# Reordering the first batch of a fused attention and feed-forward kernel: tan row by transposes, other dummy matmuls, no gates ahead of weight loads

**Chip, cores, metric.** The kernel runs on one core of a Trainium2 chip. The metric is the device time of one execution in microseconds (us), smaller is better; medians of several runs are quoted. Nearly all runs are of state "fast"; the slow ones (more than 1.5% above the fastest run of their kernel) are 7 of 19 of b_tiny, 2 of 22 of b_nogates, and one each of b_dum and b_best_slots. The ratios leave them out.

## The reference

Eight batches of eight heads, 576 positions, 64 features per head. A linear attention with cosine weights, then a feed-forward layer with 512 inputs and 2048 hidden units:

```python
theta = pi / 2 * pos / S;  c, s = cos(theta), sin(theta)
q_p = concat(relu(q) * c, relu(q) * s);  k_p = concat(relu(k) * c, relu(k) * s)
kv  = einsum('bhsf,bhsd->bhfd', k_p, v);  z = sum(k_p, axis=2)
x   = einsum('bhsf,bhfd->bhsd', q_p, kv) / (einsum('bhsf,bhf->bhs', q_p, z) + 1e-6)
h   = x @ w_in                            # (4608, 512) @ (512, 2048)
out = (h / (1 + exp(-beta * h))) @ w_out
```

## The kernel before

The matmuls of the feed-forward layer fill TensorE (PE) for most of the time: 250.8 of the span's 299.4 us by the page, and PE is busy for 96% of it in all. The attention of batch b+1 is worked in between the matmuls of a chunk of 512 tokens. Only the first batch has nothing to hide behind: loads, casts, transposes, kv products, numerators and division come one after another before the first hidden matmul can start. I call this stretch the ramp. Its order, with cuts:

```python
warm_pe(78, 40)                       # 78 dummy matmuls on zeros, 40 columns
q_relu(0, 0, "act")                   # query cast (relu, fp32 -> bf16), heads 0,1 of each half
# tan row: ones (64x128) times diag(tan), two fp32 matmuls, ACT copies to tanr
...
q_relu(0, 1, "dve")
warm_pe(5, 128)
q_turn_pe(0, 0, 4)                    # 9 transposes on PE, then ACT copies and DVE tan products
warm_pe(4, 128)
take = q_turn_pe(0, 1, 2, hold=True)
warm_pe(9)                            # 9 dummies of 512 columns
...
v_scale(0, 1, 0, eng="pool")          # v * sin on GpSimd
v_scale(0, 0, 0)                      # v * cos on DVE
k_relu(0, 0, 2, "act")                # key cast
...
kv_mm(0, 0, 6)                        # 36 matmuls: first kv product
...
nc.sync.dma_start(out=gate, in_=rk[0:1, 0, 0, 0:2])   # gate: SP waits until this key is cast
load_w("in", 1)
nc.sync.dma_start(out=gate, in_=rk[0:1, 0, 3, 0:2])   # second gate
load_w("in", 2)
load_w("in", 3)
...                                   # numerators (72 matmuls), second kv product (36),
...                                   # numerators (72), division, 8 transposes
h_mm(0, 0, (0, 1))                    # first hidden matmuls
x_turn_pe(0, 0, 4, 4, ("dve",), (1,)) # transposes of the second head pair
h_mm(0, 1, (0, 1))
x_turn_pe(0, 4, 8, 5, ("act",), (1,))
...
for i in range(1, 4):                 # DVE casts w_in blocks 1 to 3, behind the xt copies
    ... cast_win(i, gj, "dve", ...)
```

A matmul is two PE instructions, a weight load and the matmul itself (the page counts 3042 matmuls and 3068 weight loads); this will matter.

## Time and profile before

| | before |
|---|---|
| median of the three runs given | 299.19 us (298.54 to 300.53) |
| the run that was profiled | 301.22 us, span of its trace 299.4 us |
| DVE starts the w_in casts | 20.70 us |
| first w_out matmul (end of the ramp and of the first hidden tiles) | 37.81 us |

The last two rows are read from the timelines of DVE and PE. After the first w_out matmul, PE is busy nearly without a break (254.5 of the 261.2 us from 37.81 to 299.0), so what the ramp gains or loses is carried to the end. The second row deserves a look that I did not give it: the profiled run is 2 us slower than the median.

### The profile page before, as it was taken

What the parts mean: (1) busy time and instruction counts of PE and PEld (TensorE: products, weight loads), DVE (VectorE), ACT (ScalarE), POOL (GpSimd) and SP (SyncE); (2) the same over time, 40 slices, a digit from 0 to 9 for tenths busy, and PEclk for the clock granted to TensorE, in tenths of its full rate; (3) what the DMA queues carried; (4) which work ended last, traced back from release to release, by engine and by line L of the source; (5) the groups of instructions that cost most, each with busy time, mean ns of one, the idle gap of its engine ahead of it and who ended that gap; (6) DMA issues with size and microseconds to landing.
All of it is one profiled execution on the core that took longest, in us unless ns stands there. A gap on an engine that the chain in (4) does not pass through costs nothing.

```text
span 299.4 us, 7162 instructions
## 1 busy us (share of the span) xinstructions
PE 286.8 (96%) x3042; PEld 143.7 (48%) x3068; DVE 113.8 (38%) x282; ACT 141.4 (47%) x224; POOL 74.0 (25%) x88
## 2 busy tenths in 40 slices
PE   7959999999999999999999999999999999999994
PEld 6633455445544554455445544554455444444443
DVE  3869856591860077006800680059004000000000
ACT  6645765475128512860276117611761178128511
POOL 1550000516156014701270147014701210000000
PEclk9987999999999999999999999999999999999999
DMA  7999999769699349943995299419301920131032
GB/s 244 384 341 340 390 388 391 217 138 396 123 187 376 126 63 189 345 182 66 192 315 207 48 196 342 189 39 177 86 2 20 158 48 0 37 70 35 0 72 70
DMA packets 50264, 53.82 MB, mean 180 GB/s; under 512 B 30888, under 2 KB 31160, under 8 KB 50232
## 3 DMA queue, kind: packets, MB, share of 16 engines
q1 hardware_dynamic: 47512, 46.01, 51.7%
q0 software_dynamic: 2688, 7.34, 10.5%
q8 instruction: 24, 0.39, 0.6%
q14 instruction: 8, 0.07, 0.1%
q10 hardware_dynamic: 32, 0.01, 0.0%
HBM read 36.71 MB, written 9.44 MB: 154 GB/s over the span
## 4 chain that ended last, share of the span: by engine, by line
PE 92%; DVE 3%; ACT 2%; issue 1%; DVEq 0%; ACTq 0%
PE ps L374 42%; PE ps L399 40%; PE ps L289 3%; PE ps L268 3%; PE ps L415 1%; DVE qs L226 1%; PE ps L348 1%; DVE vb L213 1%; ACT g_t L381 1%; PE ps L432 1%; PE ps L238 1%; ACT xt L353 1%; ACT L151 0%; DVE xs L311 0%; PE ps L424 0%
## 5 line engine op out<-in xcount | busy, mean ns | idle before, releaser
L374 PE MATMUL ps<-xt,win 128*128 128x512 bf16 x576 | 130.4, 384 | 2.5 <-ACT xt L353 1.1
L399 PE MATMUL ps<-wout,g_t 128*128 128x512 bf16 x536 | 120.4, 379 | 2.3 <-issue 1.5
L381 ACT ACTIVATE g_t<-ps,beta 128x512 bf16<-128x512 f32 x144 | 98.7, 688 | 37.7 <-PE ps L374 37.7
L374 PEld LDWEIGHTS <-win 128*128 128x128 bf16 x576 | 56.2, 99 | 70.4 <-issue 4.3
L399 PEld LDWEIGHTS <-g_t 128*128 128x128 bf16 x560 | 53.9, 98 | 64.3 <-issue 0.5
L394 POOL DMA_DIRECT2D out_dram<-o_sb x56 | 35.3, 634 | 148.7 <-ACT o_sb L405 148.7
L405 ACT COPY o_sb<-ps 128x512 f32<-128x512 f32 x35 | 20.5, 586 | 99.6 <-PE ps L399 99.6
L226 POOL TENSOR_TENSOR qs<-qt,tanr 128x1152 bf16<-128x1152 bf16 x12 | 29.2, 2452 | 9.1 <-DVE vb L223 8.4
L280 DVE CAST kv<-ps 128x520 bf16<-128x520 f32 x7 | 4.9, 698 | 68.1 <-PE ps L268 68.1
L418 DVE COPY o_sb<-ps 128x256 f32<-128x256 f32 x1 | 0.4, 425 | 63.2 <-PE ps L415 63.2
L311 DVE TENSOR_TENSOR xs<-ps,rden 128x768 bf16<-128x768 f32 (+3 forms) x24 | 22.3, 935 | 1.0 <-DVE rden L304 0.2
L223 DVE TENSOR_SCALAR vb<-raw_v,cos 128x256 bf16<-128x256 f32 x63 | 17.1, 346 | 0.9 <-DMA raw_v<-in_v_dram 0.9
L300 DVE TENSOR_TENSOR den<-ps,eps 128x12 f32<-128x12 f32 (+3 forms) x25 | 4.1, 162 | 33.5 <-PE ps L289 33.4
L223 DVE TENSOR_SCALAR vb<-raw_v,sin 128x256 bf16<-128x256 f32 x54 | 14.7, 346 | 0.0
L289 PEld LDWEIGHTS <-qt 64*64 64x64 bf16 x576 | 10.5, 105 | 4.2 <-issue 4.2
L289 PE MATMUL ps<-kv,qt 64*64 64x65 bf16 x576 | 11.6, 195 | 0.2 <-ACT kv L278 0.2
L289 PE MATMUL ps<-kv,qs 64*64 64x65 bf16 x576 | 11.5, 193 | 0.0
L198 DVE TENSOR_SCALAR qb<-raw_q 128x1152 bf16<-128x1152 f32 x15 | 10.6, 747 | 1.3 <-DMA raw_q<-in_q_dram 1.3
L289 PEld LDWEIGHTS <-qs 64*64 64x64 bf16 x576 | 10.5, 105 | 0.0
L268 PEld LDWEIGHTS <-rk 64*64 64x64 bf16 x576 | 8.6, 106 | 3.9 <-issue 3.3
L268 PE MATMUL ps<-vb,rk 64*64 64x130 bf16 x576 | 10.2, 218 | 0.3 <-DVE vb L213 0.2
L108 DVE CAST win<-w_stage 64x512 bf16<-64x512 f32 (+2 forms) x20 | 10.0, 502 | 0.4
(58 smaller groups left out, 101.9 us busy)
## 6 DMA issues: line engine op xcount, KB each, us to landing
raw_v<-in_v_dram SPq DMA_DIRECT2D x7, 1152.0 KB, 11.4
raw_k<-in_k_dram SPq DMA_DIRECT2D x7, 1152.0 KB, 14.3
raw_q<-in_q_dram SPq DMA_DIRECT2D x7, 1152.0 KB, 7.3
out_dram<-o_sb POOLq DMA_DIRECT2D x56, 128.0 KB, 3.6
w_stage<-in_moe_w_out_dram SPq DMA_DIRECT2D x4, 1024.0 KB, 9.8
w_stage<-in_moe_w_in_dram SPq DMA_DIRECT2D x3, 1024.0 KB, 6.6
out_dram<-o_sb SPq DMA_DIRECT2D x14, 128.0 KB, 2.4
raw_q<-in_q_dram SPq DMA_DIRECT2D x2, 576.0 KB, 3.9
```

The source lines that it names most:

```text
L108: nc.vector.tensor_copy(o, a)
L198: nc.vector.tensor_scalar(dst, src, scalar1=0.0, scalar2=None, op0=ALU.max)
L223: nc.vector.tensor_scalar(o, a, scalar1=t[:, n : n + 1], scalar2=None, op0=ALU.mult)
L226: eng.tensor_tensor(dst.rearrange("q n (g p) -> q n g p", g=2), src.rearrange("q n (g p) -> q n g p", g=2), tanr[:, n0:n1].unsqueeze(2).to ...
L268: nc.tensor.matmul(t[jj * HP : (jj + 1) * HP, g], lhsT=rk[hs, n, 2 * jp + jj, :], rhs=vb[hs, n, 2 * jp + jj].rearrange("q s e -> q (s e)") ...
L289: nc.tensor.matmul(ps[cols, bank + jj, slot * E : (slot + 1) * E], lhsT=(qt, qs)[cs][rows, jp, n, cols], rhs=kv[rows, g, jp, cs, :], start ...
L311: nc.vector.tensor_tensor(o.rearrange("q j n s d -> q j (n s) d"), nv[:, :, a:z, :, 0:D].rearrange("q j n s d -> q j (n s) d"), rden[:, :, ...
L374: nc.tensor.matmul(ps[:, h_bank(c, jt)], lhsT=win[jt // 4][:, mi, (jt % 4) * P : (jt % 4 + 1) * P], rhs=xt[:, :, jp, g * HP : (g + 1) * HP ...
L381: nc.scalar.activation(g_t, ps[:, h_bank(c, jt)], AF.Silu, scale=beta[:, jt : jt + 1])
L394: eng.dma_start(out=out_v[bb, n][:, m0:m1], in_=o_sb[hf * HP : (hf + 1) * HP, m0:m1])
L399: nc.tensor.matmul(o_ps, lhsT=gs[c, jt][:, tt * P : (tt + 1) * P], rhs=wout[jt // 4][:, jt % 4, :], start=(jt == 0), stop=(jt == JT - 1))
L405: nc.scalar.copy(o_sb, o_ps)
```

## The change

The intent is to keep PE busy through the ramp, where the trace of before has the clock at 0.50 from 19.89 to 26.72 us, and to shorten the query path: the tan row comes from nine small transposes, queries are cast on VectorE, dummies fill every gap, and the weight loads are issued without waiting. The diff, cut to its core:

```diff
-    warm_pe(78, 40)
-    q_relu(0, 0, "act")
+    warm_pe(74, 32)
...
-        nc.tensor.matmul(ps[:, bank, 0 : (n1 - n0) * HP], lhsT=ones,
-                         rhs=tdiag[:, n0:n1, :], start=True, stop=True)
+        for n in range(n0, n1):
+            nc.tensor.matmul(ps[:, bank, (n - n0) * HP : (n - n0 + 1) * HP],
+                             lhsT=tan9[0:HP, n : n + 1].to_broadcast([HP, P]), rhs=identf,
+                             is_transpose=True, start=(n == n0), stop=(n == n1 - 1))
...
+    q_relu(0, 0)
...
+    warm_pe(36, 32)
+    take0 = q_turn_pe(0, 0, 4, hold=True)
+    take0("act", 0)
+    take0("act", 1)
+    take0("dve", 1)
+    q_relu(0, 1)
+    take0("dve", 0)
...
-    warm_pe(5, 128)
-    q_turn_pe(0, 0, 4)
-    warm_pe(4, 128)
+    warm_pe(24, 32)
     take = q_turn_pe(0, 1, 2, hold=True)
-    warm_pe(9)
+    warm_pe(64, 32)
+    warm_pe(5)
...
-    k_relu(0, 0, 2, "act")
+    k_relu(0, 0, 2, "act", 0, 5)
+    k_relu(0, 0, 2, "dve", 5, NQ)
...
-    nc.sync.dma_start(out=gate, in_=rk[0:1, 0, 0, 0:2])
-    load_w("in", 1)
-    nc.sync.dma_start(out=gate, in_=rk[0:1, 0, 3, 0:2])
-    load_w("in", 2)
-    load_w("in", 3)
-    warm_pe(1, bank=1)
+    for i in range(1, 4):
+        load_w("in", i)
+    warm_pe(2)
...
     x_mul(got, 0, 4)
+    x_mul(got3, 7, NQ)
     x_mul(got, 4, 7)
-    x_mul_act(got2, 7)
+    warm_pe(4, bank=3)
     h_mm(0, 0, (0, 1))
-    x_turn_pe(0, 0, 4, 4, ("dve",), (1,))
+    warm_pe(1, bank=2)
     h_mm(0, 1, (0, 1))
-    x_turn_pe(0, 4, 8, 5, ("act",), (1,))
-    x_mul_act(got2, 8)
+    x_turn_pe(0, 0, 4, 4, ("act",), (1,))
     h_mm(0, 2, (0, 1))
+    x_turn_pe(0, 4, 8, 5, ("dve",), (1,))
```

Batch 1's transposes and numerators also move one slot later in the first chunk. Also left out of the cut: two ninths of the first product of v with sin go from GpSimd to ScalarE (ACT), and the cast of the last w_out block moves two slots. I call everything above the gates the first half of the change, the rest the second half.

More of the change, by code (lines that the diff above doesn't have):

```diff
@@ L140 @@
                        allow_small_or_imprecise_dtypes=True)
+    zeros = const.tile([P, 512], BF16, name="zeros")
+    nc.vector.memset(zeros[:, 0:P], 0.0)
     halfpi = const.tile([P, 1], FP32, name="halfpi")
@@ L153 @@
     nc.scalar.activation(warm, zero_b, AF.Silu, scale=1.0)
-    zeros = const.tile([P, 512], BF16, name="zeros")
-    nc.vector.memset(zeros, 0.0)
-    ones = const.tile([HP, P], FP32, name="ones")
-    nc.vector.memset(ones, 1.0)
+    nc.vector.memset(zeros[:, P:512], 0.0)
     identf = const.tile([HP, HP], FP32, name="identf")
@@ L162 @@
     make_identity(nc, ident)
-    gate = const.tile([1, 2], BF16, name="gate")
     vb = one.tile([P, NQ, 4, 2, E], BF16, name="vb")
@@ L176 @@
     nc.vector.tensor_tensor(tan9, eps9, sin9, op=ALU.mult)
-    tdiag = const.tile([HP, NQ, HP], FP32, name="tdiag")
-    nc.vector.tensor_tensor(
-        tdiag, identf.unsqueeze(1).to_broadcast([HP, NQ, HP]),
-        tan9[0:HP].unsqueeze(2).to_broadcast([HP, NQ, HP]), op=ALU.mult)
     nc.vector.tensor_scalar(eps9, eps9, scalar1=EPS, scalar2=None, op0=ALU.mult)
@@ L427 @@
     rbeta = const.tile([P, JT], FP32, name="rbeta")
-    warm_pe(78, 40)
-    q_relu(0, 0, "act")
+    warm_pe(74, 32)
     for bank, n0, n1 in ((6, 0, 5), (7, 5, NQ)):
-        nc.tensor.matmul(ps[:, bank, 0 : (n1 - n0) * HP], lhsT=ones,
-                         rhs=tdiag[:, n0:n1, :], start=True, stop=True)
+        for n in range(n0, n1):
+            nc.tensor.matmul(ps[:, bank, (n - n0) * HP : (n - n0 + 1) * HP],
+                             lhsT=tan9[0:HP, n : n + 1].to_broadcast([HP, P]), rhs=identf,
+                             is_transpose=True, start=(n == n0), stop=(n == n1 - 1))
+    nc.tensor.transpose(ps[:, 1, 0:JT], beta16, identf[0:JT, 0:JT])
     for bank, n0, n1 in ((6, 0, 5), (7, 5, NQ)):
-        nc.scalar.copy(tanr[:, n0:n1, :].rearrange("q n p -> q (n p)"), ps[:, bank, 0 : (n1 - n0) * HP])
-    nc.tensor.transpose(ps[:, 1, 0:JT], beta16, identf[0:JT, 0:JT])
+        nc.vector.tensor_copy(tanr[:, n0:n1, :].rearrange("q n p -> q (n p)"), ps[:, bank, 0 : (n1 - n0) * HP])
+    nc.vector.tensor_copy(beta, ps[:, 1, 0:JT])
+    q_relu(0, 0)
     nc.vector.tensor_copy(ps[:, 0, 0:NQ], cos9)
     nc.vector.tensor_copy(ps[:, 0, 16 : 16 + NQ], sin9)
-    nc.vector.tensor_copy(beta, ps[:, 1, 0:JT])
+    warm_pe(36, 32)
[5 more added lines that the diff above has]
+    take0("dve", 0)
     nc.vector.reciprocal(rbeta, beta)
-    q_relu(0, 1, "dve")
-    warm_pe(5, 128)
-    q_turn_pe(0, 0, 4)
-    warm_pe(4, 128)
+    warm_pe(24, 32)
     take = q_turn_pe(0, 1, 2, hold=True)
-    warm_pe(9)
+    warm_pe(64, 32)
+    warm_pe(5)
     take("act", 0)
-    v_scale(0, 1, 0, eng="pool")
+    take("dve", 1)
+    v_scale(0, 1, 0, 0, 7, eng="pool")
+    v_scale(0, 1, 0, 7, NQ, eng="act")
     v_scale(0, 0, 0)
-    k_relu(0, 0, 2, "act")
-    take("dve", 1)
+    k_relu(0, 0, 2, "act", 0, 5)
+    k_relu(0, 0, 2, "dve", 5, NQ)
     take("dve", 0)
@@ L471 @@
         num_mm(n, 0, 2, n)
+    warm_pe(2, bank=1)
     kv_mm(0, 1, 6)
-    warm_pe(2, bank=1)
     got2 = x_rden(4, 0, 7, NQ, (0,))
@@ L479 @@
     x_mul_act(got2, 8)
+    warm_pe(2, bank=1)
     for n in range(7, NQ):
@@ L488 @@
     x_turn_pe(0, 0, 8, 2, jps=(0,))
-    got2 = x_rden(6, 0, 7, NQ, (1,))
+    got3 = x_rden(6, 0, 7, NQ, (1,))
     got = x_rden(0, 0, 0, 7, (1,))
     x_mul(got, 0, 4)
+    x_mul(got3, 7, NQ)
     x_mul(got, 4, 7)
-    x_mul_act(got2, 7)
+    warm_pe(4, bank=3)
     h_mm(0, 0, (0, 1))
-    x_turn_pe(0, 0, 4, 4, ("dve",), (1,))
+    warm_pe(1, bank=2)
     h_mm(0, 1, (0, 1))
-    x_turn_pe(0, 4, 8, 5, ("act",), (1,))
-    x_mul_act(got2, 8)
+    x_turn_pe(0, 0, 4, 4, ("act",), (1,))
     h_mm(0, 2, (0, 1))
+    x_turn_pe(0, 4, 8, 5, ("dve",), (1,))
     h_mm(0, 3, (0, 1))
@@ L530 @@
         22: lambda: (kv_mm(1, 0, 6), kv_mm(1, 1, 6), q_relu(1, 1), kv_take((0, 1), 6)),
-        24: lambda: (cast_wout(3, "aadd"), takes.append(q_turn_pe(1, 0, 4, hold=True))),
-        25: lambda: (takes.append(q_turn_pe(1, 1, 6, hold=True)),
+        25: lambda: (takes.append(q_turn_pe(1, 0, 4, hold=True))),
+        26: lambda: (takes.append(q_turn_pe(1, 1, 6, hold=True)), cast_wout(3, "aadd"),
                      [takes[jp](e, i) for jp in range(2)
                       for e, i in (("act", 0), ("dve", 1), ("act", 1), ("dve", 0))]),
-        28: lambda: (num_seven(0, 4), num_seven(1, 6), x_mul(x_rden(4, 0, 0, 7, (0,)), 0, 7)),
-        29: lambda: (x_turn_pe(1, 0, 7, 4, ("act",), (0,)), x_mul(x_rden(6, 0, 0, 7, (1,)), 0, 7)),
+        29: lambda: (num_seven(0, 4), num_seven(1, 6), x_mul(x_rden(4, 0, 0, 7, (0,)), 0, 7)),
+        30: lambda: (x_turn_pe(1, 0, 7, 4, ("act",), (0,)), x_mul(x_rden(6, 0, 0, 7, (1,)), 0, 7)),
         31: lambda: ([h_mm(1, jt, (0, 1)) for jt in range(2)], x_turn_pe(1, 0, 7, 5, ("dve",), (1,)),
```

## The prediction

> **What bounds the kernel now.** I began with the page's slices: from slice 8 on (after some 52 us) PE is at 9 in all but the last, at full clock, and no part of the change that costs much time lies there. So the case is the ramp. Next I cut the ramp into windows at the points where PE's state changes (columns: stretch, its length, busy us and instructions of PE, weight loads, DVE, ACT, POOL, granted clock, DMA share, GB/s).
>
> ```profile
> 17.07:19.80 2.73, 0.70 (x4) 0.29 (x3) 1.14 (x2) 1.43 (x3) 2.41 (x6) 1.00 0.83 249
> 19.80:22.43 2.63, 1.68 (x9) 0.97 (x9) 1.97 (x7) 0.86 (x3) 0.00 (x0) 0.52 1.05 406
> 22.43:26.72 4.29, 4.29 (x11) 1.50 (x11) 4.11 (x9) 1.52 (x3) 0.00 (x0) 0.50 1.02 359
> 26.72:37.81 11.09, 11.03 (x53) 4.94 (x52) 10.01 (x24) 9.06 (x15) 0.00 (x0) 1.00 0.99 368
> ```
>
> The reader is to see a nearly idle PE (0.70 us of 2.73), then half clock for 6.9 us. PE worked 1.68 + 4.29 = 5.97 us at half clock, so the throttle itself cost at most 5.97 / 2 = 3.0 us. Third, PE's timeline over that stretch (start, length, instruction, idle time before it and what ended it):
>
> ```profile
> 18.17 0.59 PE L374 MATMUL ps<-xt,win 128*128 128x512 bf16 x2 [1.10 <-ACT xt L353]
> 18.60 0.27 PE L348 MATMUL ps<-ident,xs 128*128 128x128 bf16 x2
> 19.86 0.40 PE L348 MATMUL ps<-ident,xs 128*128 128x128 bf16 x2 [0.99 <-issue]
> 20.05 1.06 PE L374 MATMUL ps<-xt,win 128*128 128x512 bf16 x2
> 20.90 0.63 PE L348 MATMUL ps<-ident,xs 128*128 128x128 bf16 x4
> 22.43 5.72 PE L374 MATMUL ps<-xt,win 128*128 128x512 bf16 x16 [0.89 <-ACT xs L321]
> ```
>
> Three gaps: 1.10 us for an xt copy, 0.99 us for "issue" in the middle of four transposes, and 0.89 us for the ACT piece of the last division. Fourth, DVE over the same stretch: it waits for those transposes, copies xt, and then casts weights without a break.
>
> ```profile
> 20.36 0.42 DVE L355 COPY xt<-ps 128x512 bf16<-128x512 bf16 x1 [2.15 <-PE ps L348]
> 20.70 10.45 DVE L108 CAST win<-w_stage 64x256 bf16<-64x256 f32 x20
> ```
>
> The casts end at 31.15, while the last four hidden tiles start at about 37.81 - 4 x 0.864 = 34.4 us (0.864: four matmuls at 0.216 apart; w_out matmuls start at 37.81). So DVE has 3.2 us of slack, and that is all that a faster PE can take before it waits for casts.
>
> The 0.99 us on issue needs an owner. Both transposes after it carry no wait. The page's DMA table has a queue of instructions; the same view in windows of 0.3 us finds its first fetches at 11.4, 17.4, 23.8 and 47.6 us (the first two shown).
>
> ```profile
> q8 instruction: 24, 0.39, 0.6%
> ...
> q8 instruction: 1, 0.02, 20.4%
> ...
> q8 instruction: 1, 0.02, 23.0%
> ```
>
> 24 fetches of 16 KB against 3042 + 3068 PE instructions: 6110 / 24 = 255 each. Counting PE's records, the stall falls after the 703rd. Going back 256 gives number 447, where the first numerator matmuls stop from 13.61 to 13.74, and 191, passed at 8.3. The fetch after each comes late: 8.3 to 11.4, 13.7 to 17.4, 19.9 to 23.8, so 3.1 to 3.9 us[...], lasts 1.0 to 1.1, and PE goes on 1.3 us after its end (12.4 to 13.74, 18.5 to 19.86). A block of 256 PE instructions thus cannot be had in the ramp in less than 5.5 to 6.1 us. I hold this for the owner of that gap; it is a reading of three coincidences, not proved.
>
> [...]
>
> **The change, part by part.**
> 1. Tan row. Out go tdiag (0.75 us on DVE) and a ones matmul, four passes from 4.29 to 6.58. In come nine fp32 transposes. From the one weight load of that kind, 0.18 to 0.33 us, I estimate 0.21 x 9 = 1.9 us, from 3.45 (tan ready 3.38) to about 5.5. Copies go from ACT to DVE (2 x 0.4). Gain in the row: about 1 us, but only 0.4 us at the first query transpose (7.54 to about 7.1), as DVE now has the copies, the beta copy and the query cast (0.69, ACT took 1.16) in line.
> 2. The rest of the head before 14 us gains nothing at the end: the last key piece lands at 13.93 us (ACT waits 0.38 for it) and kv of the second head pair cannot be done before about 15.1; it is done at 15.24 now. 0.1 us at most.
> 3. Dummies. Before: 99 in the whole ramp. After: 74 + 36 + 24 + 64 tiny and 16 long, 214 in all. Tiny ones are cheap in time (0.036 us each at 40 columns) but each is two instructions.
> 4. The last division moves from ACT to DVE: removes the 0.89 us gap, adds some 0.3 us on DVE.
> 5. Without gates the DMA dip at 17.0 to 18.5 (149 GB/s against 385: 0.9 us of transfer) goes. The w_in casts never waited for a landing beyond the first block, so this moves no cast; later loads land up to 0.9 us sooner.
> 6. Batch 1's transposes one slot later: nothing in itself; it fits a PE that runs ahead of the loads by a slot or more.
>
> If all gaps and the throttle go: transposes end by about 19.3, casts run from 19.6 to 30.0, w_out begins by 30.0 + 4 x 0.864 = 33.5, so 4.3 us sooner. The loads give part of it back: DVE's cast of the last w_out block waits for its landing until 46.78, about 45.9 without the dip, and 2.8 us of tan products (four of 0.7) follow before batch 1's numerators. Those then start near 49.9 against 51.38 now; some is made good by matmuls that run meanwhile. I put the net of this course at 2.5 us.
>
> **Rivals.** First, **instruction supply becomes the wait**. In the new order the counts are: 148 after the first 74 dummies, 168 after tan and beta, 240 after 36, 452 after the 64, 686 at the second kv product, 948 to 960 at the last query-side transposes. So boundary 191 falls in the 36 dummies (about 6.4 us), 447 in the 64 (about 11.8), and 703 in the second kv product, which has its data at 14.5. By 5.5 to 6.1 us per block, 703 is not to be had before 17.3 to 18.3: kv ends 2 to 3 us later than now, the boundary at 959 comes up at 23.5 to 24.5, the casts start at about 23.8 to 24.7 and w_out at about 37.8 to 38.7: between no gain and 0.9 us lost[...]. For: the two stalls of the kernel before fit to a tenth. Against: the fetch delay came from three cases, and the counts look tuned on the chip. Second, **DVE becomes the bound**: it has more work ahead of its casts, and they set the end of the hidden tiles in either course; already counted above. Third, **the gain is hidden by the loads** at 45 to 50 us, as the move by a slot suggests: the gain then shrinks towards 1 us.
>
> **Range and chances.** I give the full course (-2.5 us) 0.4, the instruction course (about 0 to +1.5, mean +0.7) 0.45, the part swallowed by loads (-1) 0.15: -1.0 + 0.3 - 0.15 = -0.85, taken as -1.0: 299.2 - 1.0 = **298.2 us**. The range runs from 0.9 us beyond the first course to the instruction course with the throttle: 295.8 to 300.9. A change of 2% is 6.0 us, more than the ceiling of 4.3 and more than any loss above, so within 2% has 0.94, each side 0.03.
>
> **What would show it.** The clock at 1.00 through 17 to 38 us shows the dummies right. A gap of PE on issue inside the second kv product (k matmuls with vb) shows the instruction rival, its absence refutes it. The start of the w_in casts (20.70 now) and of the w_out matmuls (37.81 now) give the net of the ramp, and the w_out start less the total's change gives what the loads took back. I am wrong if fetches are faster in the new order (then nearer 296.5), or if stalls pile up at both boundaries (above 300).

## The result

The changed kernel takes 304.14 us in the median (303.53 to 304.88, 4 runs), the kernel before 299.86 us in the same rounds (298.54 to 300.57, 4 runs). The ratio is 1.0149, with a 95% interval from 1.0101 to 1.0197: some 4.4 us slower. Ratios here are the mean time of one kernel's fast runs over that of the other's of the same rounds, so not quite the ratio of the medians.

First, four windows of the changed kernel over its ramp (columns as in the prediction: stretch, length, busy us and instructions of PE, weight loads, DVE, ACT, POOL, clock, DMA share, GB/s):

```profile
17.09:18.66 1.57, 0.21 (x5) 0.05 (x5) 1.50 (x4) 0.00 (x0) 1.41 (x4) 1.00 1.04 387
18.66:24.01 5.35, 5.06 (x126) 3.09 (x128) 2.29 (x8) 2.50 (x7) 0.64 (x2) 1.00 0.81 298
24.01:25.14 1.13, 0.23 (x4) 0.06 (x2) 0.00 (x0) 0.30 (x1) 0.00 (x0) 1.00 0.08 25
25.14:40.22 15.08, 13.43 (x63) 5.58 (x63) 14.25 (x32) 10.21 (x16) 0.00 (x0) 1.00 0.73 268
```

The clock is at 1.00 throughout, as the change intended. Yet there are two stretches with a nearly idle PE, and in the second almost nothing is busy: DMA moves 25 GB/s. PE's timeline of the changed kernel names them (start, length, instruction, idle time before and its end):

```profile
14.62 0.42 PE L260 MATMUL ps<-vb,rk 64*64 64x130 bf16 x16 [0.89 <-DVE rk L190]
...
16.78 0.52 PE L260 MATMUL ps<-vb,rk 64*64 64x130 bf16 x7
18.66 0.64 PE L260 MATMUL ps<-vb,rk 64*64 64x130 bf16 x29 [1.36 <-issue]
...
23.96 0.28 PE L340 MATMUL ps<-ident,xs 128*128 128x128 bf16 x2
25.14 0.29 PE L340 MATMUL ps<-ident,xs 128*128 128x128 bf16 x2 [0.90 <-issue]
...
28.90 0.82 PE L366 MATMUL ps<-xt,win 128*128 128x512 bf16 x3 [0.50 <-DVE win L108]
...
33.52 6.86 PE L366 MATMUL ps<-xt,win 128*128 128x512 bf16 x31 [0.88 <-DVE win L108]
40.22 4.05 PE L391 MATMUL ps<-wout,g_t 128*128 128x512 bf16 x17
```

The second kv product stops after seven of its matmuls, in the middle of a run that waits for no engine, until 18.66 us; the last transposes stop halfway until 25.14. Both gaps are "issue": PE waited for no engine that the profile shows. The page's DMA table counts one instruction fetch more than before, 25 against 24 (queue, number, MB, share):

```profile
q8 instruction: 25, 0.41, 0.6%
```

The later waits for DVE (0.50 and 0.88 us) are for w_in casts. DVE and POOL (GpSimd) of the changed kernel:

```profile
12.22 2.34 DVE L190 TENSOR_SCALAR rk<-raw_k 128x512 bf16<-128x512 f32 x1
...
25.53 0.42 DVE L347 COPY xt<-ps 128x512 bf16<-128x512 bf16 x1 [2.92 <-PE ps L340]
25.87 10.44 DVE L108 CAST win<-w_stage 64x256 bf16<-64x256 f32 x20
```

```profile
12.16 2.11 POOL L205 TENSOR_TENSOR vb<-raw_v,sin 128x1152 bf16<-128x1152 f32 x1 [1.04 <-DMA raw_v<-in_v_dram]
```

DVE of the kernel before, its cast of 320 key columns:

```profile
14.01 0.48 DVE L198 TENSOR_SCALAR rk<-raw_k 128x320 bf16<-128x320 f32 x1
```

Two things are to be seen. The casts start at 25.87 us, 5.2 us later than in the trace of before, and end at 36.3; PE waits for them, and the first w_out matmul comes at 40.22 (37.81). And a key cast of 512 columns took 2.34 us on DVE, where 320 columns took 0.48 before: it started 0.06 us after a GpSimd product and ended 0.3 us after that product's end. At the rate of the 320 columns (1.5 ns each), 512 would take 0.77 us: an estimate. Not every DVE instruction beside a GpSimd product is slow in this trace: the second query cast, begun at 8.83 us, 0.16 us ahead of one, took 0.75 us. What holds up the cast at 12.22 us is not shown.

The profiled spans differ by 2.9 us (302.3 against 299.4), the medians by 4.3. The reason is the trace of before: its run took 301.22 us. In all 20 kernels of this study, the time of the profiled run less the start of its first w_out matmul lies between 263.3 and 265.5 us (before: 301.22 - 37.81 = 263.4; changed: 304.04 - 40.22 = 263.8). A median run of before (299.2) should then start w_out near 299.2 - 264 = 35.2 us: an estimate, but b_slots, whose ramp is the same code, has 35.17 in a run of 299.13. So the change moved this start not by 2.4 us but by 5.

### The profile page after: what moved, and what is told of

The parts are those of the page before. It is cut to its first block, busy times and chain, and to the rows that moved or that the text cites. A ratio compares the mean times of both kernels' runs of the same rounds, so it can differ in the third digit from the quotient of the medians.

```text
span 302.3 us, 7396 instructions
## 1 busy us (share of the span) xinstructions
PE 285.8 (95%) x3161; PEld 144.1 (48%) x3188; DVE 117.0 (39%) x286; ACT 138.2 (46%) x219; POOL 75.2 (25%) x88
## 4 chain that ended last, share of the span: by engine, by line
PE 89%; DVE 6%; issue 2%; ACT 2%; ACTq 0%; DVEq 0%
PE ps L366 39%; PE ps L391 39%; PE ps L281 4%; PE ps L260 3%; DVE win L108 2%; PE ps L407 1%; PE ps L416 1%; DVE rk L190 1%; PE ps L340 1%; DVE qs L218 1%; ACT xt L345 1%; PE ps L230 1%; ACT L153 0%; ACT g_t L373 0%; DVE vb L205 0%
## 5 line engine op out<-in xcount | busy, mean ns | idle before, releaser
L366 PE MATMUL ps<-xt,win 128*128 128x512 bf16 x576 | 128.6, 379 | 2.5 <-DVE win L108 1.4
L366 PEld LDWEIGHTS <-win 128*128 128x128 bf16 x576 | 55.3, 98 | 70.0 <-DVE win L108 3.3
L386 POOL DMA_DIRECT2D out_dram<-o_sb x56 | 36.4, 654 | 150.9 <-ACT o_sb L397 150.9
L303 DVE TENSOR_TENSOR xs<-ps,rden 128x768 bf16<-128x768 f32 (+4 forms) x25 | 22.7, 914 | 0.8
L190 DVE TENSOR_SCALAR rk<-raw_k 128x2304 bf16<-128x2304 f32 (+2 forms) x9 | 12.3, 1364 | 0.6 <-DMA raw_k<-in_k_dram 0.6
L190 DVE TENSOR_SCALAR qb<-raw_q 128x1152 bf16<-128x1152 f32 x16 | 11.4, 751 | 1.3 <-DMA raw_q<-in_q_dram 1.3
L416 PE MATMUL ps<-zeros 128*128 128x32 bf16 (+1 forms) x211 | 9.8, 196 | 1.8 <-DVE zero_b L146 1.0
```

Source lines behind the costliest of these rows:

```text
L190: nc.vector.tensor_scalar(dst, src, scalar1=0.0, scalar2=None, op0=ALU.max)
L303: nc.vector.tensor_tensor(o.rearrange("q j n s d -> q j (n s) d"), nv[:, :, a:z, :, 0:D].rearrange("q j n s d -> q j (n s) d"), rden[:, :, ...
L366: nc.tensor.matmul(ps[:, h_bank(c, jt)], lhsT=win[jt // 4][:, mi, (jt % 4) * P : (jt % 4 + 1) * P], rhs=xt[:, :, jp, g * HP : (g + 1) * HP ...
L386: eng.dma_start(out=out_v[bb, n][:, m0:m1], in_=o_sb[hf * HP : (hf + 1) * HP, m0:m1])
L416: nc.tensor.matmul(ps[:, bank, 0:w], lhsT=zeros[:, 0:P], rhs=zeros[:, 0:w], start=True, stop=True)
```

## The experiments

Two theories stood at first. **F**: PE's instructions come in blocks of 256 (an estimate: 6110 of them against 24 fetches are 255 each), a block takes about 6 us to come in during the ramp (the prediction's 5.5 to 6.1 us, from three fetches in the trace of before), and the added dummies use up blocks. Its rivals **L** and **D**: the order of work on DVE (for L, the cast of 2.34 us) holds up the ramp, and dummies cost their time only. Labels that begin with a_ are edits of the changed kernel, with b_ of the kernel before. Each was run in five rounds or more against the kernel before (median 299.1 to 299.5 in the rounds of every set).

### Set 1: key cast, and tiny against long dummies

a_kact:
```diff
-    k_relu(0, 0, 2, "act", 0, 5)
-    k_relu(0, 0, 2, "dve", 5, NQ)
+    k_relu(0, 0, 2, "act")
```


> The changed kernel with the first key cast whole on ACT again, so that no DVE cast runs beside the GpSimd product. Theory F (PE instruction supply sets the ramp): the first kv product is done about 1 us sooner, but the stall on issue inside the second kv product still ends at 18.7 us (+-0.3), the w_in casts still start at 25.9 (+-0.4) and the time stays within 0.7 us of the changed kernel. Rival L (the 2.34 us DVE cast beside GpSimd is what delays the ramp): the second kv product is done 2 us sooner, casts start near 24, time 1.5 to 2 us lower.

Measured: 303.98 us (changed 304.14). The stall in the second kv product ended at 18.83 us, the casts started at 25.76. These are F's numbers; L had casts near 24. One part of F's expectation missed: the first kv product was not done 1 us sooner, but 0.4 us later (15.42 against 15.04 us). The reason makes the run a weak test of L: the overlap did not vanish, it moved. With the key cast gone, the second query cast on DVE fell into GpSimd's product and took 1.85 us instead of 0.75. a_mended below is the clean test.

a_long:
```diff
-    warm_pe(36, 32)
+    warm_pe(5, 448)
-    warm_pe(24, 32)
+    warm_pe(3)
-    warm_pe(64, 32)
+    warm_pe(8)
```


> The changed kernel with its three groups of tiny dummies (124) replaced by 16 long ones of the same PE time; 216 PE instructions fewer. Theory F: no stall on issue inside the second kv product, which then is done near 17.5 us (limited by the DVE order); the stall moves to the last transposes of the first head pair and ends there near 22 us; casts start near 25, time 0 to 1.5 us lower. Rival D (the order of work on DVE and ACT delays the ramp, dummies do not matter): the gap in the second kv product stays or turns into a wait for DVE of the same length, casts at 25.9, time the same.

Measured: 306.83 us, slower instead of faster. PE's timeline of this kernel:

```profile
16.67 0.92 PE L260 MATMUL ps<-vb,rk 64*64 64x130 bf16 x36
...
18.80 0.45 PE L340 MATMUL ps<-ident,xs 128*128 128x128 bf16 x5
22.14 0.34 PE L340 MATMUL ps<-ident,xs 128*128 128x128 bf16 x3 [2.89 <-issue]
```

The place was right: the kv product runs through all 36 matmuls, the stall is in the first head pair's transposes and ends at 22.14 (expected near 22). The size was wrong: the stall was 2.9 us long, the clock was half from 23.7 to 27.1 us, the last transposes and the first hidden matmuls mostly ran at that clock, and the casts started at 27.82, not 25.

a_kact_long is both edits. 

> Both edits. Theory F: second kv product done near 15.5 to 16 us without a stall on issue, then one stall on issue at the last transposes of the first head pair until about 21 us (fetch asked for near 15 plus 6.1); casts near 24, time 1 to 2.5 us lower than the changed kernel[...]. Rivals L and D: as the key cast alone (about -2 us), with no such stall.

Measured: 306.85 us. The stall stood in the same transposes, until 24.06 us, casts at 29.35. Again the place was as F has it and the time was not; the second query cast was again slow (1.55 us against 0.75).

b_tiny:
```diff
-    warm_pe(9)
+    warm_pe(72, 32)
```


> The kernel before with its nine long dummies replaced by 72 tiny ones of the same PE time; 126 PE instructions more, nothing else. Theory F: a stall on issue of about 0.5 us near the start of the first numerators (until 13.7 us) and one of about 3.5 us inside the second numerators (until about 19.9 us), the old stall at the transposes gone; casts start near 23.5 (20.7 before), time 1 to 2.5 us longer than before. Rival (instruction count does not matter, only the time that dummies take): no new gap, time within 0.5 us of before.

Measured: 303.26 us in the median of 19 runs, but in two groups: 3 runs at 299.4 to 299.7 and 16 at 302.3 to 304.8. Seven of the 16 count as slow; the ratio of the other 12 runs is 1.0075 (1.0040 to 1.0111). So more instructions in the same PE time cost time, as F says, but not in every run. The trace taken is of the fastest run, in the quicker group: a stall inside the second numerators was there, but only from 15.82 to 17.18 us, and the casts started at 20.71. The slow group has no trace, so how its 3 us arise stays open.

### What the traces of all kernels say of the stall

Counting PE's records (weight loads and matmuls) from the start, the stalls on issue fall at the same count, after 697 to 700, whatever work stands there (some records are missing; the prediction also counted PE's few semaphore instructions, which makes it 703 both before and in the changed kernel). 14 of the 20 traces have such a stall; the other six come there 1.2 us or more after the fetch's end. The table gives, for seven of the 14, the time of record 444 (256 earlier), the second fetch of instructions among the trace's DMA packets, and the time at which PE goes on at about record 700.

| kernel | work at record 700 | record 444 | second fetch | PE goes on | after the fetch's end |
|---|---|---|---|---|---|
| before | last transposes | 13.61 | 17.41 to 18.52 | 19.86 | 1.34 |
| changed | second kv product | 11.63 | 16.28 to 17.38 | 18.66 | 1.28 |
| a_long | first pair's transposes | 15.91 | 19.52 to 20.62 | 22.14 | 1.52 |
| a_kact_long | first pair's transposes | 17.91 | 21.54 to 22.62 | 24.06 | 1.43 |
| b_tail (below) | dummies | 15.10 | 18.64 to 19.73 | 21.15 | 1.42 |
| a_mended (below) | second kv product | 10.42 | 14.57 to 15.53 | 16.93 | 1.40 |
| b_dum (below) | dummies | 14.72 | 17.38 to 18.40 | 19.73 | 1.33 |

From record 444 to record 700 it takes 5.0 to 7.0 us in these. In all 14, PE goes on 1.3 to 1.6 us after the fetch's end. A stall at one instruction count across several kinds of work, ended 1.3 to 1.6 us after a 16 KB fetch, is hard to have from anything but instruction supply; that is an inference from these counts and times.

What holds the fetch back was not measured, and its delay is no constant: record 444 comes at 13.72 us in a_gates and at 13.76 in b_tail_nodum, both with gates, but the second fetch starts at 14.77 in the one and at 16.94 in the other. In both, it starts where the loads thin out: the DMA share falls from 0.94 to 0.46 at 14.5 us, and from 1.17 to 0.40 at 17.0. In the changed kernel the third fetch starts at 22.55 us, where the share falls from 0.99 to 0.43; but its second fetch, at 16.28, started at a share of 1.12. So a pause in the loads goes with a fetch in some of these traces, not in all; no run tests it.

### Set 2: the halves of the change, and the count alone

b_head is the first half alone (the code from the gates on as before). 

> Only the first half of the change (tan row, dummies, casts and order up to the last key cast), with the second half as before (gates, ACT pieces of the last division, its dummies). Theory F: the stall near PE record 700 sits inside the second kv product again and ends at 18.7 +- 0.5 us, casts start near 25.5, time near that of the changed kernel or worse: 304 to 306 us. Rival G (the missing gates or the dummies of the second half cost the time): near before, 299 to 301.

Measured: 301.46 us (ratio 1.0079, 1.0049 to 1.0108), a miss: I had expected 304 to 306. Rival G, with 299 to 301, missed too. Of the stall in the second kv product only 0.3 us are left, at a weight load after record 699: the second fetch ran at 14.38 us, not 16.28, though record 444 came at 11.64, as in the changed kernel. This trace also has half clock from 11.6 to 15.0 us.

b_tail is the second half alone. 

> Only the second half of the change (no gates, division on DVE, dummies in its gaps, batch 1 one slot later), with the head as before. Theory F: no stall inside the kv products; the stall near record 700 stays after 18 us, casts start at 20 to 21, the throttle stays away: time 297 to 299.5 us, as before or up to 2 us less. Rival G: 302 or more.

Measured: 303.38 us (ratio 1.0146): the larger miss, and the rival's number. PE's timeline:

```profile
17.74 0.62 PE L348 MATMUL ps<-ident,xs 128*128 128x128 bf16 x8
21.15 0.82 PE L424 MATMUL ps<-zeros 128*128 128x512 bf16 x3 [2.79 <-issue]
21.81 0.59 PE L374 MATMUL ps<-xt,win 128*128 128x512 bf16 x2
```

The stall is there at its count, but it now stands ahead of all hidden matmuls, in the middle of the dummies that were put there; it ends 1.3 us later than before, and the remaining three dummies (0.65 us) go first. Casts start at 24.38. Each half alone costs (2.2 and 4.1 us in the medians), and together they cost little more than the second alone (4.4): I take it that they draw on the same wait, which no run shows by itself. The difference between the two second fetches (14.38 with gates, 16.28 without, record 444 at 11.64 and 11.63) gave a new theory, **FG**: a fetch waits behind the outstanding loads, and the gates kept these few. It is a guess from these two traces; set 3 is to test it.

b_align:
```diff
-    warm_pe(78, 40)
+    warm_pe(68, 46)
```


> The kernel before with its first 78 dummies of 40 columns as 68 of 46: the same PE time and 20 instructions fewer, nothing else. Theory F: the block boundary moves 20 instructions down the work: the stall leaves the last transposes for the hidden matmuls after them, casts start near 19.8 (20.7 before), in return 0.3 to 0.5 us of stall inside the second kv product; time 0 to 1.5 us less. Rival (dummies matter by their time alone): no difference in the places of the gaps.

Measured: 298.56 us (ratio 0.9978, 0.9955 to 1.0000). The gaps at the transposes moved as expected: all eight transposes of the second head pair now end before record 700, and the casts start at 19.77. The stall of 0.3 to 0.5 us that I expected in the second kv product is not there (36 matmuls in 0.70 us). The gain is small and just at the edge of the noise.

b_best is this with 66 dummies of 47 columns, the two ACT pieces of the division on DVE as in the change, and one matmul of fp32 operands ahead of the hidden ones:
```diff
+    x_mul(got3, 7, NQ)
...
-    x_mul_act(got2, 7)
+    nc.tensor.matmul(ps[:, 3, 0:320], lhsT=ones, rhs=tdiag[:, 0:5, :], start=True, stop=True)
...
-    x_mul_act(got2, 8)
```


> The kernel before with 66 dummies of 47 columns (24 instructions fewer), the last division's two ACT pieces on DVE as in the change, and one fp32 matmul (4 instructions, some 1.1 us of PE) in the gap ahead of the hidden matmuls. Theory F: no stall before the hidden matmuls, no 0.9 us wait for ACT, throttle rarer: casts start near 20, time 296.5 to 298.5 us, 1 to 3 us under before. Rival: within 0.7 us of before.

Measured: 297.70 us (ratio 0.9968, 0.9946 to 0.9990), casts at 19.23 us. The matmul of fp32 operands, two PE matmuls in the trace, took 0.80 us. It beats both kernels, by little.

### Set 3: the gates

a_gates puts the two gate transfers back into the changed kernel. 

> The changed kernel with the two gates ahead of the w_in loads put back, nothing else. Theory FG (a fetch of PE instructions waits behind the loads that are outstanding, and without gates more of them are): the second fetch starts near 14.4 us instead of 16.3, block 3 is there by 16.8, so the stall on issue inside the second kv product goes or shrinks below 0.5 us; casts start near 22 (25.9), time 300 to 302 us, 2 to 4 under the changed kernel. Rival (instruction count alone, gates immaterial): stall to 18.7 as before, time 303.5 to 305.

Measured: 302.42 us, 1.7 under the changed kernel. The second fetch ran at 14.77 us and no stall showed in the second kv product. The casts start at 23.76, not 22. In this trace the second query cast took 2.27 us beside a GpSimd product, so that PE came to record 444 only at 13.72 us; that may hold the gain down, but a_mended below, without it, is no faster.

b_nogates takes the gates away from the kernel before. 

> The kernel before with the gates taken away, nothing else. Theory FG: the second fetch starts 0.7 to 1.5 us later after its boundary than with gates, the stall near record 700 ends near 21 instead of 19.9, casts start 1 to 3 us later; time 301 to 304 us. Rival: time within 0.7 us of before.

Measured: 300.29 us (ratio 1.0026, 1.0002 to 1.0050): the sign is right, the size is near the rival's 0.7 us, and FG's own number failed: from record 444 to the second fetch it took 3.4 us (12.95 to 16.34), against 3.8 with gates in the kernel before. The trace is of the fastest of the 22 runs (297.70 us); the stall stands at the same two transposes, with 0.24 us of idle PE until 18.72. So the size is not explained.

b_tail_gates is the second half with gates. 

> The second half of the change alone, but with the gates kept. Theory FG: the 4 us of that half are the gates: time 297.5 to 300 us, stall near record 700 under 1.5 us. Rival (its dummies, DVE division or slot move cost the time): 302 to 304.5.

Measured: 301.93 us: gates bring 1.5 of the 4 us, not all; a miss. The trace of this kernel has a stall of 2.3 us among the added dummies, then half clock (from 21.27 us on, two hidden matmuls take 1.06 us instead of 0.59); in b_tail the stall was 2.79 us long and the hidden matmuls after it took 0.59. From record 444 to the second fetch it is 3.3 us, and 3.5 in b_tail without gates, so in this pair the fetch delay does not account for the 1.5 us.

a_mended is a_gates with the key cast on ACT and the second query cast ahead of the tan product:
```diff
-    take0("dve", 1)
     q_relu(0, 1)
+    take0("dve", 1)
```


> The changed kernel with gates back, the first key cast whole on ACT and the second query cast ahead of the tan product that it stood behind, so that no DVE cast falls into a GpSimd product. Theory FG[...]: the second kv product done by 15.5 to 16 us, casts start at 20.5 to 21.5; time 297.5 to 300.5 us. If gates alone do not help, 303 or more.

Measured: 302.74 us, a miss. No DVE cast of this part fell into a GpSimd product any more and the first kv product was done 1.9 us sooner than in the changed kernel, yet the time is that of a_gates. PE's timeline shows where the gain went:

```profile
14.88 0.30 PE L261 MATMUL ps<-vb,rk 64*64 64x130 bf16 x7
16.93 0.64 PE L261 MATMUL ps<-vb,rk 64*64 64x130 bf16 x29 [1.75 <-issue]
```

PE arrived sooner at record 700 and waited longer there (the second fetch still ran only at 14.57 us); half clock followed, from 17.5 to 20.9 us; casts at 24.31. So the slow cast is a true cost on DVE (1.9 us at the first kv product) that is hidden behind the stall on issue (1.75 us here).

### Set 4: what is left of the second half

b_dum adds to the kernel before only the second half's eight dummies:
```diff
-    warm_pe(1, bank=1)
+    warm_pe(2)
...
+    warm_pe(2, bank=1)      # ahead of the second kv product
-    warm_pe(2, bank=1)      # behind it
+    warm_pe(2, bank=1)      # ahead of the second numerators
...
+    warm_pe(4, bank=3)
     h_mm(0, 0, (0, 1))
+    warm_pe(1, bank=2)
```


> The kernel before with only the second half's eight added dummies (one more ahead of the numerators, the others moved or added ahead of the hidden matmuls: 16 PE instructions). Theory F: they push the boundary near record 700 up the work to just ahead of the hidden matmuls, so that all transposes of the second head pair come after the stall, and what is left of the dummies then stands in front of them at half clock: casts start at 23 to 24.5 (20.7), time 301 to 303 us. Rival (it is the division on DVE or the slots that cost): time within 0.7 us of before.

Measured: 300.53 us (ratio 1.0039, 1.0015 to 1.0062; one run of 310 is not among the fast ones), casts at 21.87. The stall sits in the dummies as expected, with half the expected cost.

b_tail_nodum is b_tail_gates without them. 

> The second half of the change with the gates kept and without its added dummies: division on DVE, xt copies swapped, batch 1 one slot later. Theory F: casts start at 19.5 to 21, time 298 to 299.8 us, at or under before. Rival: 301 to 303.

Measured: 298.93 us (ratio 0.9998). Taking eight dummies away gave 3.0 us, and left 0.33 us of the 2.3 us stall. The division on DVE, the swapped copies and the slot move cost nothing together.

b_slots is the kernel before with the slot move alone. 

> The kernel before with batch 1's transposes and numerators one slot later, nothing else. Ramp the same up to 44 us; I expect the time within 0.6 us of before, since the stalls at 53 and 60 us wait for DVE and not for the slot.

Measured: 298.85 us (ratio 1.0005). Nothing, as expected.

b_best_slots is b_best with the slot move. 

> The aligned kernel (24 instructions fewer, division on DVE, one fp32 matmul) with batch 1 one slot later. In that kernel PE stood 1.5 us at 43 us for batch 1's query load, which the later slot should hide: 296.5 to 297.7 us, 0 to 1.2 us under the aligned kernel. If the slot move only moves the wait: the same as the aligned kernel, 297.7.

Measured: 298.55 us (ratio 0.9976; one run of 601 us left out), not better than b_best: the wait at 43 us (1.2 us in b_best) did go, but PE is idle for 0.5 us at 49 us (0.7 in b_best) and for 0.1 to 0.2 us at 47 and 53.

### Set 5: the change's work without its dummies

a_lean is a_mended with 82 dummies instead of 214:
```diff
-    warm_pe(74, 32)
+    warm_pe(61, 50)
-    warm_pe(36, 32)
+    warm_pe(5, 128)
-    warm_pe(24, 32)
+    warm_pe(4, 128)
-    warm_pe(64, 32)
-    warm_pe(5)
+    warm_pe(9)
...                      # and the eight dummies of the second half out
```


> The changed kernel with its tan row, its casts and its DVE division, but gates back, the key cast on ACT, the second query cast in front of the tan product, and the dummies cut to 82 (61 of 50 columns, 5 and 4 of 128, 12 of 512), so that the last transposes of the second head pair end before PE instruction 700. Theory F (what counts is how many PE instructions lie ahead of those transposes): no stall ahead of them, casts start at 19.3 to 20.3, time 296.8 to 298.8 us, 4 us under the mended kernel that has the same work. Rival (the new tan row or the query cast on DVE costs the time): 301 or more.

Measured: 298.28 us (ratio 0.9960, 0.9941 to 0.9979), 4.5 us under a_mended. PE's and DVE's timelines of this kernel:

```profile
19.06 0.39 PE L341 MATMUL ps<-ident,xs 128*128 128x128 bf16 x4
19.28 0.59 PE L367 MATMUL ps<-xt,win 128*128 128x512 bf16 x2
19.71 0.39 PE L341 MATMUL ps<-ident,xs 128*128 128x128 bf16 x4
19.94 0.59 PE L367 MATMUL ps<-xt,win 128*128 128x512 bf16 x2
```

```profile
20.21 0.42 DVE L348 COPY xt<-ps 128x512 bf16<-128x512 bf16 x1 [1.62 <-PE ps L341]
20.55 10.43 DVE L108 CAST win<-w_stage 64x256 bf16<-64x256 f32 x20
```

The eight transposes run without a stall; the weight load of the last is record 693 of PE (956 in the changed kernel), and the casts start at 20.55. That is 0.25 us later than expected; the time is inside what was expected. Against a_mended both the number of dummies and the PE time that they take differ, so the number alone is told by b_tiny and b_align, which keep the time (as does a_long, where fewer instructions cost 2.7 us: what counts is the work on which the boundary falls); a_lean tells that the tan row, the query casts on DVE and the division together cost nothing against the kernel before.

a_lean_nogates is the same without gates. 

> The same without gates. Theory F: with the critical transposes ahead of the boundary, later fetches lie behind the casts, so the gates matter less than the 1.5 us that they were worth in the changed kernel: within 1 us of the same kernel with gates.

Measured: 298.70 us (ratio 0.9978). Gates are worth 0.4 us here, against 1.7 in the changed kernel. That fits a slow fetch hurting only the work that stands behind a boundary.

## Why the prediction was wrong

The measured 304.14 lies above the range of 295.8 to 300.9. The course that came about was one that the text had, its first rival; its place was right and its size and its weight were not. The step that failed is the full course, "if all gaps and the throttle go", which had 0.4 and set the sign: the throttle did go (clock 1.00), but the gaps did not. PE stood 1.36 and 0.90 us on issue, and w_out began at 40.22 us, not at 33.5. Step by step:

- **The owner of the 0.99 us gap** was right. The count at which PE stalls stayed at 703 (counted as in the prediction) while the work there changed.
- **The place of the stalls** was right: second kv product at 703 (seen: 17.09 to 18.66 us) and last transposes at 959 (seen: 24.01 to 25.14).
- **The size of the rival** was too small. PE was to pass 703 at 17.3 to 18.3 us and did so at 18.66; 959 at 23.5 to 24.5, and did so at 25.14; the casts were to start at 23.8 to 24.7 and came at 25.87; w_out was put at 37.8 to 38.7. Two terms were mis-sized. The fetch delay was taken as 3.1 to 3.9 us from the kernel before; without gates the second one was 4.3 to 4.7 us (11.63 or 11.99 to 16.28). And the second query cast was queued behind a tan product, which the text did not have, so that the second query transposes began at 9.64 us (8.93 before).
- **Part 5 failed outright.** "This moves no cast; later loads land up to 0.9 us sooner" looked only at data. Gates put back were worth 1.7 us in the changed kernel and 1.5 in the second half alone. In the changed kernel the second fetch then ran at 14.77 us and not at 16.28; for the second half the way in which gates help stays open.
- **Part 3 failed in part.** It counted the dummies as instructions, but gave the long ones no cost of their own. The second half's eight of them cost 3.0 us beside the rest of that half, and 1.5 alone.
- **Parts 1 and 2** put the head's gain too low in its own place: the nine tan transposes took 1.19 us (1.9 put), and the first query transposes began at 6.28 us (7.1 put, 7.54 before). That none of it would be left at the second kv product was right, but for another reason than the landing of the last key piece: the product ended at 19.3 us, behind the stall.
- **Parts 4 and 6** were right: the 0.89 us wait for ACT went, DVE's division cost nothing (b_tail_nodum), nor did the slots (b_slots).
- **The base was the wrong run.** The 3.0 us of throttle and the 37.81 us of the w_out start were read from a run of 301.22 us and subtracted from a median of 299.19. A median run starts w_out near 35.2 us (b_slots: 35.17), so much of the gain that I hoped for had already been in the median. The w_out start of 37.8 to 38.7 us that the rival named meant 302 to 303 us (plus the 264 of above, an estimate), not 299 to 300.
- **The chances**: 0.4 for the full course rested on the look of tuned counts, which is no evidence in a trace; and the sum of -0.85 was rounded to -1.0. Within 2% held.

What stays open: why b_tiny has two groups of times; why removing the gates costs the kernel before only 0.8 us in the ratio; and what holds an instruction fetch back. One clue to the first: eight kernels share the opening of the kernel before. In six of their traces the first clock record comes at 9.65 to 12.80 us and the first nine query transposes take 0.96 us to start; in b_tiny and b_nogates, traced in the fastest run of each, it comes at 3.92 and 4.70 us and they take 0.51. Whether the clock was late in the runs that took longer is not recorded.

## What to carry to other kernels

A dummy matmul costs two instructions besides its time (before: 3042 matmuls, 3068 weight loads). Where PE stands on issue at one instruction count, as here after 697 to 700 records, count the dummies ahead of the critical work, and end that work before the count: in a_lean the last of those transposes is record 693, and the time is 4.5 us under a_mended. When a wait is on issue at the same instruction count in two versions, look at the instruction queue of the DMA view (here PE went on 1.3 to 1.6 us after a fetch's end), and try the loads at another time: gates put back brought 1.7 us in the changed kernel, 0.4 in a_lean. And before reading a gain from a profile, compare the time of the profiled run with the median (here 301.22 against 299.19 us).

## What the traces show of fetches and of the clock

- PE stood on issue in the ramp: 0.99 us before, 1.36 + 0.90 us in the changed kernel, 2.89 us in a_long. PE went on at about record 700 soon after the end of a fetch that started after record 444. That this fetch brings the work from record 700 on is an estimate from these counts and times.
- From record 444 to the start of the second fetch it took 1.1 to 4.2 us in the 13 kernels with gates (median 2.7) and 3.0 to 4.7 in the 7 without (median 3.5), then 0.9 to 1.1 us for 16 KB. Where there was a stall, it was 1.3 to 1.6 us more until PE went on.
- With the same 78 dummies from 1.25 us on, the trace's first clock record came at 3.92 us in b_tiny, 4.70 in b_nogates, 9.65 in the kernel before and 12.80 in b_tail. The profile's clock row shows full speed ahead of that record, but the transposes tell: nine of them took 0.96 us to start in the kernel before and 0.50 in b_best (66 dummies), where the record came at 4.96. What sets the time of that record was not tested.

Kernel before, PE's timeline (the nine transposes end where the next dummies start):

```profile
7.54 1.17 PE L238 MATMUL ps<-ident,qb 128*128 128x128 bf16 x9
8.50 0.63 PE L424 MATMUL ps<-zeros 128*128 128x128 bf16 x4
```

b_best, the same:

```profile
6.54 0.67 PE L238 MATMUL ps<-ident,qb 128*128 128x128 bf16 x9
7.04 0.39 PE L424 MATMUL ps<-zeros 128*128 128x128 bf16 x4
```
